# Windowed attention ahead of two feed-forward nets: global keys between K^T's blocks, quarter-array products in two banks, ten weight pieces begun in listed steps

## The chip, the core and the metric

The kernel runs on one core of one Trainium2 chip. The metric is the device time of one execution in microseconds. The core has five engines that each run their own list in order: PE (TensorE, with its weight loads shown as PEld), DVE (VectorE), ACT (ScalarE), POOL (GpSimd) and SP, which here only issues transfers. All numbers are fp32.

## The reference, cut to what matters

Four batches, eight heads, 512 local and 32 global positions per head, head size 64. A local query sees the keys within 32 positions and the 32 global keys; a global query sees all 544 keys. The 2176 x 512 result goes through two nets of width 2048.

```python
k_all = np.concatenate([k_g, k_l], axis=2)
out_g = np.matmul(sm(scale * np.matmul(q_g, k_all.transpose(0, 1, 3, 2))), v_all)
s_ll  = np.where(np.abs(pos[:, None] - pos[None, :]) <= 32, scale * q_l @ k_l.T, -1e9)
a_l   = sm(np.concatenate([scale * q_l @ k_g.T, s_ll], axis=-1))
out_l = np.matmul(a_l, np.concatenate([v_g, v_l], axis=2))
x = concat([out_g, out_l], axis=2).transpose(0, 2, 1, 3).reshape(2176, 512)
x = (h * cos(h)) @ w_out      with h = x @ w_in        # first net
y = relu(h)**2 @ w_out        with h = x @ w_in        # second net
```

## The kernel before, in words

**Items and steps.** The attention is cut into 40 items: 32 `Local` ones (a pair of heads and one half of the 512 positions) and 8 `Global` ones (four heads), always four Locals and then a Global. Steps -3 to 43 run through them. In each step the list `CFG["order"]` sets in which order the stages are written, and `CFG["lag"]` says for which item: S (scores) for item s, SM (maxima on DVE, exponentials on ACT) for s, RC and NM (reciprocal; scaling, most of it on POOL) for s-1, TM (transposes of the probabilities on PE) for s-2, TE (their copies out of PSUM, by ACT) for s-3, OM and OE (products with V, and the copy of the result) for s-4. Global items stand at the steps 4, 9, 14 and so on. Each engine runs its part strictly in the order written.

**K^T.** `tr_k` (TRK) transposes the keys of a head pair, `k_evac` (KEV, ACT) copies them as eight blocks of 64 into `kT`, eight rows of 160: block, next block, 32 global keys. `k_copy` (KC, POOL) fills the other two parts: line 351 copies the next blocks (448 columns), line 353 the global keys (256 columns), line 361 the last 64 keys.

**Products.** `o_mm` makes two 128-column halves `i`. For each it issues two products with the global values (line 504: 128 rows against 64 columns of the array, 128 columns wide) and four with the local values (line 516). Results of one item lie in one of the banks 6 and 7, in turn, and `o_evac` copies 256 columns with one DVE instruction (line 529), after NM and the weight conversion in DVE's order.

**Loads.** SP issues K loads (LK) in the steps 0, 5, 10, ... 25, Q loads (LQ) in 1, 6, 11, ... 26, V loads (LV) in 8, 13, ... 33, and copies of V shifted by 64 rows (CV) in 11, 16, ... 36; every tenth step from 5 on it also loads `vgz`.

**Weights.** The nets' weights come in 64 pieces of 512 KB. `Feed.begin` issues the load of a piece (`raw`) and shifts a list of stages: two steps later ACT and POOL read it (`conv_a`, lines 146 and 143), three steps later DVE (`conv_b`, lines 154 and 155), four steps later POOL (`conv_c`, line 165). `begin` stands (BG) behind LQ and TE, ahead of LK and of the exponentials. Before, half a credit per step from step 5 on, with none in the steps five ahead of a head pair, begins pieces in the steps 8, 11, 14, 18, 21, 24, 28, 31, 34, 36 and 38, and from step 40 on one in nearly every step. `Feed.split`, in listed steps, makes two-part weights of converted pieces.

From step 40 on `ffn_step` runs the nets as well: products `h` (line 757) and `y` (line 786).

Of the kernel before, what the change touches and what calls it, by code (L numbers as in the profile page):

```python
# [26 lines left out]
           'RC', 'NM', 'CB', 'LV', 'OE', 'TRQ', 'QE', 'KC', 'TM'],  # L27
# [19 lines left out]
 'free': -5,  # L47
 'kb': 'P',
 'split': [22, 24, 27, 29, 33],
 'sx': [32, 34, 37, 39],  # L50
 'arate': 0.5,
 'rate': 0.5,
 's0': 5,
# [6 lines left out]
RATE, ARATE, XD, NRING = CFG["rate"], CFG["arate"], CFG["xd"], CFG["nr"]  # L60

@with_exitstack
def kernel(
# [250 lines left out]
    def load_vg(b):  # L314
        for u in range(4):
            nc.sync.dma_start(
                VGZ[b % 2][32 * u : 32 * u + 32, :, u, :],
                v_g[b].rearrange("(k h) p d -> p k h d", h=2)[:, :, u // 2, :],
            )

    def tr_k(p):
        b, kk = divmod(p, NPAIR)
        tk = bank(BT, "tk")
        for c in range(4):
            nc.tensor.transpose(  # L325
                tk[:, c * P : (c + 1) * P],
                kn[p // 2][:, c, 2 * (p % 2) : 2 * (p % 2) + 2].rearrange("p h d -> p (h d)"),
                ident,
            )
        t = ep.tile([P, 8, KTB], F32, tag="kT", name="kT", bufs=3)  # L330
        kT[p] = t
        tks[p] = tk

    def k_evac(p):
        t, tk = kT[p], tks.pop(p)
        nc.scalar.activation(
            t[:, :, 0:64], tk.rearrange("p (j q) -> p j q", q=64), AF.Copy
        )
        if CFG["kb"] == "A":
            nc.scalar.activation(  # L340
                t[:, :, 128:KTB], tk[:, 0:SG].unsqueeze(1).to_broadcast([P, 8, SG]), AF.Copy
            )
        elif CFG["kb"] == "D":
            nc.vector.tensor_copy(
                t[:, :, 128:KTB], tk[:, 0:SG].unsqueeze(1).to_broadcast([P, 8, SG])
            )

    def k_copy(p):
        t = kT[p]
        one = dict(scalar1=1.0, scalar2=1.0, op0=ALU.mult, op1=ALU.mult)  # L350
        nc.gpsimd.tensor_scalar(t[:, 0:7, 64:128], t[:, 1:8, 0:64], **one)
        if CFG["kb"] == "P":
            nc.gpsimd.tensor_scalar(
                t[:, :, 128:KTB], t[:, 0, 0:SG].unsqueeze(1).to_broadcast([P, 8, SG]), **one
            )
        if p > 1:
            k_tail(p)

    def k_tail(p):
        b, kk = divmod(p, NPAIR)  # L360
        nc.gpsimd.tensor_scalar(
            kT[p][:, 7, 64:128], ktail[:, kk, b, :], 1.0, 1.0, op0=ALU.mult, op1=ALU.mult
        )
# [41 lines left out]

    class Local:
# [19 lines left out]

        def softmax(self):
            self.pt = lp.tile([P, 4, KTB], F32, tag="pt", name="pt", bufs=4)  # L430
            self.st = lp.tile([P, 3, 4], F32, tag="st", name="st", bufs=4)

            def unit(u):
                i = 2 * self.hb + u % 2
                m = masks[1] if i == 0 else masks[2] if i == 3 else masks[0]
                nc.vector.tensor_tensor_reduce(  # L436
                    out=self.pt[:, u, :],
                    in0=self.s[u // 2][:, 160 * (u % 2) : 160 * (u % 2) + 160],
                    in1=m,
                    scale=-0.125,  # L440
                    scalar=3.0e38,
                    op0=ALU.add,
                    op1=ALU.min,
                    accum_out=self.st[:, 0, u : u + 1],
                )
# [9 lines left out]
            return [lambda u=u: unit(u) for u in range(4)]  # L455
# [10 lines left out]
        def norm(self):  # L466
# [3 lines left out]
                self.pt[:, :, P:KTB],  # L470
# [54 lines left out]
        def o_evac(self):  # L525
            c0 = self.b * SL + 256 * self.hb
            dst, src = xt[:, self.kk, c0 : c0 + 256], self.o.rearrange("p i q -> p (i q)")
            if CFG["oe"][self.hb] == "D":
                nc.vector.tensor_copy(dst, src)
            else:  # L530
                nc.scalar.activation(dst, src, AF.Copy)


    class Global:
# [3 lines left out]
        def s_mm(self):  # L538
            self.s = []
            for n in (320, 256):  # L540
                s = bank(BT if CFG["sgb"] >> (n == 256) & 1 else BS, "sg")
                self.s.append(s)
                for i in range(2):
# [5 lines left out]
                        rhs=t[:, 0:5, 0:64] if n == 320 else t[:, 5:8:2, 0:128],  # L549
# [64 lines left out]
        def o_mm(self):  # L614
            self.o = bank(BO, "og")[:, 0 : 2 * SG].rearrange("p (i q) -> p i q", i=2)
# [33 lines left out]
    for h in range(2):  # L649
# [6 lines left out]
            out=masks[0][s, 64:128], in_=masks[0][s, 64:128], pattern=[[-1, 64]],  # L656
# [5 lines left out]
    nc.vector.memset(masks[2][64:128, 96:128], NEG)  # L662
# [361 lines left out]
```

## Time and profile before

| what | us |
|---|---|
| three runs, median (lowest to highest) | 913.23 (912.32 to 914.58) |
| the profiled execution's own time | 911.74 |
| its span, first to last instruction | 910.0 |
| PE busy in the span | 890.7 |
| DVE, ACT, POOL busy | 502.5, 439.4, 447.8 |
| first product of the nets starts at | 146.06 |

Busy is time in which an engine has an instruction in hand; it doesn't say that the engine is at its best rate. What counts for the end is in which stretch PE has to wait, or has work that could be shorter. PEclk is the share of the full TensorE clock that was granted: 1.00 is 2.4 GHz, 0.5 is 1.2 GHz.

### The profile page before, as it was taken

To read this page: it belongs to the slowest core of one execution; us is meant where nothing else is said; L and a number is where in the kernel's file an instruction comes from. 1 tells how busy PE (TensorE), PEld (TensorE's weight loads), DVE (VectorE), ACT (ScalarE), POOL (GpSimd) and SP (SyncE) were. 2 spreads that over 40 slices of the span, in tenths; PEclk is the share of its full clock that TensorE was granted. 3 is DMA by queue.
4 is the path that set the end of the run, shared out by engine and by line. 5 is a ranking of instruction groups with operands and counts; after the bars stand their busy time and mean duration, and the time that the engine had idled before them with its cause. 6 is when DMAs were issued, how large, how long until landed. Compare 5 with 4: busy or idle time off the path is not lost.

```text
span 910.0 us, 15436 instructions
## 1 busy us (share of the span) xinstructions
PE 890.7 (98%) x5720; PEld 793.7 (87%) x5720; DVE 502.5 (55%) x1058; ACT 439.4 (48%) x1036; POOL 447.8 (49%) x517
## 2 busy tenths in 40 slices
PE   7899999999999999999999999999999999999997
PEld 5777777999999999999999988889999888899996
DVE  5687899866776666765554483433422833232221
ACT  5778787665655545545444553333334632222211
POOL 4577888754574435744342484444423842222221
PEclk9999999999999999999999999999999999999999
DMA  7888643221122111121110021111100101010001
GB/s 168 192 192 195 165 129 94 71 70 53 49 62 70 47 53 61 50 70 47 47 47 1 1 70 47 53 44 66 47 1 1 47 1 47 1 47 1 35 35 36
DMA packets 82075, 57.10 MB, mean 63 GB/s; under 512 B 58320, under 2 KB 74704, under 8 KB 82000
## 3 DMA queue, kind: packets, MB, share of 16 engines
q1 hardware_dynamic: 79824, 55.59, 22.0%
q8 instruction: 45, 0.74, 0.3%
q10 hardware_dynamic: 2176, 0.52, 0.3%
q14 instruction: 30, 0.25, 0.1%
HBM read 47.45 MB, written 4.46 MB: 57 GB/s over the span
## 4 chain that ended last, share of the span: by engine, by line
PE 91%; DVE 3%; DMA 2%; ACT 1%; SPq 1%; POOL 1%; issue 1%; ACTq 0%; POOLq 0%; DVEq 0%
PE h L757 41%; PE y L786 41%; PE s L420 2%; PE tw L488 1%; PE o L504 1%; PE tq L368 1%; DVE pt L436 1%; PE o L516 1%; PE og L622 1%; DMA raw<-in_moe_w_out_dram 1%; PE sg L546 1%; PE tk L325 0%; ACT pt L446 0%; SPq L292 0%; PE twg L603 0%
## 5 line engine op out<-in xcount | busy, mean ns | idle before, releaser
L757 PE MATMUL h<-x,w 128*128 128x436 f32 (+3 forms) x1920 | 403.4, 358 | 0.0
L857 POOL TENSOR_TENSOR glo<-cr,ghi 128x436 fp32r<-128x436 f32 (+3 forms) x160 | 186.8, 1167 | 407.7 <-ACT ghi L851 393.9
L757 PEld LDWEIGHTS h<-x,w 128*128 128x128 f32 x1920 | 354.6, 188 | 27.5
L786 PE MATMUL y<-ghi,w 128*128 128x436 f32 (+1 forms) x640 | 177.6, 358 | 0.0
L846 DVE TENSOR_TENSOR cr<-h,cr 128x436 f32<-128x436 f32 (+3 forms) x160 | 96.6, 605 | 134.0 <-ACT cr L837 115.0
L786 PE MATMUL y<-w,ghi 128*128 128x512 f32 x544 | 168.4, 390 | 0.0
L745 DVE TENSOR_TENSOR x<-xt,x 128x436 fp32r<-128x436 f32 (+3 forms) x100 | 102.5, 1035 | 93.3 <-ACT x L744 78.3
L837 ACT ACTIVATE cr<-h 128x384 f32<-128x384 f32 (+1 forms) x80 | 42.8, 535 | 210.7 <-PE h L757 209.4
L786 PEld LDWEIGHTS y<-ghi,w 128*128 128x128 f32 x640 | 120.3, 188 | 6.1
L786 PEld LDWEIGHTS y<-w,ghi 128*128 128x128 f32 x544 | 101.4, 188 | 18.9
L786 PE MATMUL y<-glo,w 128*128 128x436 f32 (+1 forms) x320 | 114.8, 359 | 0.0
L786 PE MATMUL y<-w,glo 128*128 128x512 f32 x272 | 106.8, 393 | 0.0
L851 ACT ACTIVATE ghi<-cr 128x436 fp32r<-128x436 f32 (+3 forms) x160 | 89.7, 560 | 24.5 <-DVE cr L846 23.6
L831 ACT ACTIVATE ck<-h 128x436 int32<-128x436 f32 (+1 forms) x80 | 42.6, 532 | 113.1 <-PE h L757 113.1
L833 DVE SCALAR_TENSOR_TENSOR cr<-h,ck 128x436 f32<-128x436 f32 (+1 forms) x80 | 48.6, 607 | 84.9 <-ACT ck L831 84.9
L165 POOL TENSOR_TENSOR r<-cu,cc 128x512 uint32<-128x512 uint32 x64 | 85.0, 1328 | 2.0 <-DVE cc L155 2.0
L744 ACT ACTIVATE x<-xt 128x436 fp32r<-128x436 f32 (+3 forms) x100 | 55.1, 560 | 20.2 <-PE h L757 19.9
L786 PEld LDWEIGHTS y<-glo,w 128*128 128x128 f32 x320 | 60.1, 188 | 2.7
L786 PEld LDWEIGHTS y<-w,glo 128*128 128x128 f32 x272 | 51.0, 188 | 10.8
L842 ACT ACTIVATE cr<-cr,halfpi 128x436 f32<-128x436 f32 (+1 forms) x80 | 52.5, 657 | 10.1 <-DVE cr L833 10.1
L155 DVE SCALAR_TENSOR_TENSOR cc<-raw,cc 128x512 uint32<-128x512 uint32 x64 | 55.7, 870 | 0.0
L446 ACT ACTIVATE pt<-pt,st 128x160 f32<-128x160 f32 x128 | 53.3, 425 | 4.1 <-DVE st L436 4.1
(91 smaller groups left out, 907.4 us busy)
## 6 DMA issues: line engine op xcount, KB each, us to landing
raw<-in_moe_w_in_dram SPq DMA_DIRECT2D x32, 512.0 KB, 3.7
raw<-in_moe_w_out_dram SPq DMA_DIRECT2D x32, 512.0 KB, 3.5
vb<-va SPq DMA_DIRECT2D x16, 256.0 KB, 4.6
out_dram<-ypart SPq DMA_DIRECT2D x16, 256.0 KB, 2.1
qn<-in_q_l_dram SPq DMA_DIRECT2D x28, 128.0 KB, 3.7
va<-in_v_l_dram SPq DMA_DIRECT2D x24, 128.0 KB, 3.3
kn<-in_k_l_dram SPq DMA_DIRECT2D x21, 128.0 KB, 3.0
va<-in_v_l_dram SPq DMA_DIRECT2D x8, 96.0 KB, 3.2
```

Of the source, the lines that this page charges most:

```text
L155: lambda: v.scalar_tensor_tensor(c, t[:, :, 1].bitcast(U32), 0x80000000, c, op0=ALU.bitwise_and, op1=ALU.bitwise_or,),
L165: nc.gpsimd.tensor_tensor(ring[g][:, q, :].bitcast(U32), u, c, op=ALU.add)
L446: nc.scalar.activation(self.pt[:, u, :], self.pt[:, u, :], AF.Exp, bias=self.st[:, 0, u : u + 1], scale=-1.0, accum_out=self.st[:, 1, u : ...
L744: nc.scalar.activation(hi, xr, AF.Copy)
L745: return lambda: (nc.vector if kk in XD else nc.gpsimd).tensor_tensor(lo, xr, hi.bitcast(F32), op=ALU.subtract)
L757: nc.tensor.matmul(h, lhsT=w[:, ws, 0, kk * P : (kk + 1) * P], rhs=x, start=(k == 0), stop=(k == 3 * NK - 1),)
L786: nc.tensor.matmul(o, lhsT=l, rhs=r, start=(c_first and k == 0), stop=(c_last and k == 2))
L833: lambda: nc.vector.scalar_tensor_tensor(r, h, INV2PI, k, op0=ALU.mult, op1=ALU.subtract),
L842: nc.scalar.activation(ctmp[s], ctmp[s], AF.Sin, bias=halfpi, scale=TWOPI)
L846: nc.vector.tensor_tensor(r, hps.pop(s), r, op=ALU.mult)
L851: nc.scalar.activation(ghi[s], ctmp[s], AF.Copy)
L857: nc.gpsimd.tensor_tensor(lo, ctmp.pop(s), hi.bitcast(F32), op=ALU.subtract)
```

## The change

**K^T** becomes nine rows of 96: block, 32 global keys. A query block's 160 keys are then one contiguous run, block j, global keys, block j+1, so line 351 goes, and the masks and the slices of the probabilities move with it. The scaled probabilities go to a tile of their own, `pn`, and `pt` has three buffers of five rows.

**Products.** The four products with the global values come first, each on 64 rows and 64 columns of the array; the two row halves write different banks. Each item now uses a 128-column half of both banks 6 and 7, and the halves alternate. `o_evac` is two copies of 128 columns, and OE moves ahead of RC, right behind the maxima.

**Weights.** Pieces begin in the ten steps listed under `begin`, and none at BG from step 37 on. The split steps are 15, 21, 25, 31 and 35.

```diff
@@ CFG
- 'order': [... 'SM', 'RC', 'NM', 'CB', 'LV', 'OE', 'TRQ', 'QE', 'KC', 'TM'],
+ 'order': [... 'SM', 'OE', 'RC', 'NM', 'CB', 'LV', 'TRQ', 'QE', 'KC', 'TM'],
- 'split': [22, 24, 27, 29, 33],
+ 'split': [15, 21, 25, 31, 35],
- 'arate': 0.5,
+ 'begin': [6, 9, 14, 16, 19, 24, 26, 29, 34, 36],
@@ pools
+    obank = [ps.tile([P, 512], F32, tag=f"bank{k}", name="o") for k in BO]
+    def out_half():
+        k = turn["o"] = turn.get("o", 1) ^ 1
+        return [t[:, P * k : P * k + P] for t in obank]
+    GK = slice(64, 64 + SG)
@@ k_copy
-        nc.gpsimd.tensor_scalar(t[:, 0:7, 64:128], t[:, 1:8, 0:64], **one)
-        if CFG["kb"] == "P":
-            nc.gpsimd.tensor_scalar(
-                t[:, :, 128:KTB], t[:, 0, 0:SG].unsqueeze(1).to_broadcast([P, 8, SG]), **one
-            )
+        nc.gpsimd.tensor_scalar(
+            t[:, 0:8, GK], t[:, 0, 0:SG].unsqueeze(1).to_broadcast([P, 8, SG]), **one
+        )
@@ Local.s_mm
-                            rhs=kT[self.p][d, j, :],
+                            rhs=kT[self.p].rearrange("p j q -> p (j q)")[d, 96 * j : 96 * j + KTB],
@@ Local.norm
+            self.pn = lp.tile([P, 4, P], F32, tag="pn", name="pn", bufs=2)
-                    self.pt[:, u, 0:P],
-                    self.pt[:, u, 0:P],
+                    self.pn[:, u].rearrange("p (a q) -> p a q", a=2),
+                    windows(self.pt, u),
@@ Local.o_mm
-            self.o = bank(BO, "o")[:, 0:256].rearrange("p (i q) -> p i q", i=2)
+            self.o = out_half()
             for i in range(2):
+                r = slice(64 * i, 64 * i + 64)
                 for h in range(2):
                     nc.tensor.matmul(
-                        self.o[64 * h : 64 * h + 64, i, :],
-                        lhsT=VGZ[self.b % 2][:, self.kk, 2 * h + i, :],
-                        rhs=self.tgs,
+                        self.o[i][64 * h : 64 * h + 64],
+                        lhsT=VGZ[self.b % 2][r, self.kk, 2 * i + h, :],
+                        rhs=self.tgs[r],
@@ Local.o_evac
-            dst, src = xt[:, self.kk, c0 : c0 + 256], self.o.rearrange("p i q -> p (i q)")
-            if CFG["oe"][self.hb] == "D":
-                nc.vector.tensor_copy(dst, src)
+            for i in range(2):
+                nc.vector.tensor_copy(xt[:, self.kk, c0 + P * i : c0 + P * i + P], self.o[i])
@@ steps
-                cb = feed.begin(ARATE if due(CFG["free"]) is None else 0.0) if s >= CFG["s0"] else []
+                cb = feed.begin(1.0 if s in CFG["begin"] else 0.0)
```

SP's list before, from the Q loads (`qn`) of step 6 on; `raw` is the first weight piece, begun in step 8, `va` the V loads of step 8:

```order
L292 DMA qn<-in_q_l_dram 128x4x64 x4
L397 DMA qgn<-in_q_g_dram 32x8x64
L126 DMA raw<-in_moe_w_in_dram 128x4x256
L299 DMA va_85<-in_v_g_dram 32x4x64
L302 DMA va_85<-in_v_l_dram 96x4x64
```

The same stretch of SP's list now:

```order
L299 DMA qn<-in_q_l_dram 128x4x64 x4
L124 DMA raw<-in_moe_w_in_dram 128x4x256
L394 DMA qgn<-in_q_g_dram 32x8x64
L306 DMA va_87<-in_v_g_dram 32x4x64
L309 DMA va_87<-in_v_l_dram 96x4x64
```

The first piece moved ahead of one 64 KB load, and is issued right behind the four Q loads of step 6, not ahead of them.

ACT's list before, from the copies (`tws`, `tgs`) of step 8 on; the exponentials are `pt`, `cc` is the first reader of `raw`:

```order
L494 ACTIVATE tws<-tw 128x512
L498 ACTIVATE tgs<-tg 128x128
L446 ACTIVATE pt,st<-pt,st 128x160 x4
L494 ACTIVATE tws<-tw 128x512
L498 ACTIVATE tgs<-tg 128x128
L336 ACTIVATE kT<-tk 128x8x64
L571 ACTIVATE ptg,stg<-sg,stg 128x320
L571 ACTIVATE ptg,stg<-sg,stg 128x224
L494 ACTIVATE tws<-tw 128x512
L498 ACTIVATE tgs<-tg 128x128
L146 ACTIVATE cc<-raw 128x512
```

ACT's list now, from the same copies of step 8 on:

```order
L498 ACTIVATE tws<-tw 128x512
L502 ACTIVATE tgs<-tg 128x128
L144 ACTIVATE cc<-raw 128x512
L449 ACTIVATE pt,st<-pt,st 128x160 x4
L498 ACTIVATE tws<-tw 128x512
L502 ACTIVATE tgs<-tg 128x128
L343 ACTIVATE kT<-tk 128x8x64
L574 ACTIVATE ptg,stg<-sg,stg 128x320
```

The reader of the first piece moved two steps up, from step 10 to step 8, ahead of that step's exponentials.

PE's list before, a step with a Local's scores (`s`), its products (`o`) and the transposes of Q (`tq`), with waits:

```order
L420 MATMUL s<-kT,qT 64x160 x6
L504 MATMUL o<-tgs,vgz_89 64x128 x2
L516 MATMUL o<-tws,va_86 64x64 [waits DMAHW5_49]
L516 MATMUL o<-tws,va_86 64x64
L516 MATMUL o<-tws,vb_88 64x64 x2
L504 MATMUL o<-tgs,vgz_89 64x128 x2
L516 MATMUL o<-tws,va_86 64x64 x2
```

The same step now:

```order
L423 MATMUL s<-kT,qT 64x160 x6
L509 MATMUL o<-tgs,vgz_91 64x128 [waits DVE_49]
L509 MATMUL o<-tgs,vgz_91 64x128
L509 MATMUL o<-tgs,vgz_91 64x128 [waits DVE_49]
L509 MATMUL o<-tgs,vgz_91 64x128
L522 MATMUL o<-tws,va_88 64x64 [waits DMAHW5_49]
L522 MATMUL o<-tws,va_88 64x64
```

The four products with the global values stand together, and the first of each bank has a wait on DVE that was not there.

## Rows read from the trace of the kernel before

**Rows 1.** Busy time by stretch (us: engine busy (instructions), PEclk, DMA share, GB/s)

```profile
core 0: us, PE busy (x) PEld busy (x) DVE busy (x) ACT busy (x) POOL busy (x), PEclk, DMA share, GB/s
20.00:33.00 13.00, 10.46 (x149) 8.17 (x152) 8.51 (x45) 8.16 (x33) 6.21 (x16) 1.00 0.88 197
...
42.00:59.00 17.00, 15.78 (x254) 12.59 (x253) 13.10 (x63) 13.34 (x51) 11.83 (x27) 1.00 0.87 196
59.00:75.00 16.00, 16.00 (x258) 13.07 (x257) 13.41 (x64) 12.95 (x51) 13.39 (x27) 1.00 0.91 201
...
126.00:143.00 17.00, 14.85 (x241) 11.27 (x239) 16.32 (x68) 13.77 (x52) 14.72 (x26) 1.00 0.41 125
...
161.00:910.00 749.00, 743.93 (x3651) 678.11 (x3649) 375.38 (x540) 319.76 (x609) 332.06 (x288) 1.00 0.13 42
```

**Rows 2.** Chain that ended last, one Local's products (start us, us, what)

```profile
66.42 0.37 PE o L504 x4
...
67.02 0.22 PE o L504 x4
```

**Rows 3.** Groups by line (busy us, mean ns | idle before, releaser)

```profile
L529 DVE COPY xt<-o 128x256 f32<-128x256 f32 x32 | 13.2, 413 | 1.4 <-PE o L516 1.4
...
L351 POOL TENSOR_SCALAR kT<-kT 128x448 f32<-128x448 f32 x16 | 9.4, 588 | 4.5 <-ACT kT L336 4.5
...
L633 DVE COPY xt<-og 128x64 f32<-128x64 f32 x8 | 1.7, 214 | 0.0
```

**Rows 4.** Timeline of PE and POOL at the nets' start (start, us, what, idle before)

```profile
145.87 0.33 PE L488 MATMUL tw<-ident,pt 128*128 128x128 f32 x1 [0.37 <-POOL pt L475]
...
143.71 2.10 POOL L475 TENSOR_SCALAR pt<-pt,st 128x128 f32<-128x128 f32 x3
```

**Rows 5.** Timeline of ACT, step 13: the reader of a piece waits

```profile
55.92 0.69 ACT L146 ACTIVATE cc<-raw 128x512 uint32<-128x512 uint32 x1 [2.17 <-DMA raw<-in_moe_w_out_dram]
```

**Rows 6.** Timeline of SP, Q loads of step 6 and the first piece

```profile
34.75 2.59 SPq L292 DMA_DIRECT2D qn<-in_q_l_dram  x4
...
37.94 1.34 SPq L126 DMA_DIRECT2D raw<-in_moe_w_in_dram  x1
```

**Rows 7.** Tile raw, the one load issued between 37.5 and 39 us

```profile
DMA to landing us min/median/max: 5.1/5.1/5.1
```

**Rows 8.** Timeline of ACT, behind step 8's copies and step 9's copy

```profile
38.06 0.43 ACT L446 ACTIVATE pt<-pt,st 128x160 f32<-128x160 f32 x1
...
39.71 0.59 ACT L494 ACTIVATE tws<-tw 128x512 f32<-128x512 f32 x1
```

**Rows 9.** Timeline of PE, step 9's transposes

```profile
41.72 0.60 PE L488 MATMUL tw<-ident,pt 128*128 128x128 f32 x4
```

**Rows 10.** Timeline of SP, Q loads of step 16

```profile
65.94 3.09 SPq L292 DMA_DIRECT2D qn<-in_q_l_dram  x4
```

**Rows 11.** Tile raw, the one load issued at 69.75 us

```profile
DMA to landing us min/median/max: 5.2/5.2/5.2
```

**Rows 12.** Timeline of ACT, behind step 18's copies

```profile
70.88 0.43 ACT L446 ACTIVATE pt<-pt,st 128x160 f32<-128x160 f32 x1
```

**Rows 13.** Timeline of SP and ACT, step 26's Q loads and step 28's copies

```profile
98.61 3.27 SPq L292 DMA_DIRECT2D qn<-in_q_l_dram  x4
...
105.57 0.42 ACT L446 ACTIVATE pt<-pt,st 128x160 f32<-128x160 f32 x1
```

**Rows 14.** Busy time in a stretch with the lower clock (columns as in rows 1)

```profile
87.00:92.00 5.00, 4.51 (x35) 3.32 (x37) 3.03 (x10) 3.45 (x13) 2.65 (x8) 0.66 0.68 153
```

**Rows 15.** Timeline of SP and ACT, the piece begun in step 21

```profile
81.92 0.50 SPq L126 DMA_DIRECT2D raw<-in_moe_w_in_dram  x1
...
87.49 0.67 ACT L146 ACTIVATE cc<-raw 128x512 uint32<-128x512 uint32 x1
```

**Rows 16.** Timeline of DVE, step 12's last maximum

```profile
50.70 0.32 DVE L436 CUSTOM_DVE_ANT_0 pt<-s,mask 128x160 f32<-128x160 f32 x1
```

**Rows 17.** Timeline of PE, step 13's scores

```profile
51.30 0.77 PE L420 MATMUL s<-kT,qT 64*64 64x160 f32 x16
```

More of the change, by code (lines that the diff above doesn't have):

```diff
@@ L26 @@
 CFG = {'order': ['CV', 'LQ', 'S', 'TE', 'BG', 'LK', 'OM', 'TRK', 'KEV', 'CC', 'SM',
-           'RC', 'NM', 'CB', 'LV', 'OE', 'TRQ', 'QE', 'KC', 'TM'],
+           'OE', 'RC', 'NM', 'CB', 'LV', 'TRQ', 'QE', 'KC', 'TM'],
  'lag': {'S': 0,
@@ L46 @@
  'teg': 'AA',
- 'free': -5,
  'kb': 'P',
- 'split': [22, 24, 27, 29, 33],
+ 'split': [15, 21, 25, 31, 35],
  'sx': [32, 34, 37, 39],
- 'arate': 0.5,
+ 'begin': [6, 9, 14, 16, 19, 24, 26, 29, 34, 36],
  'rate': 0.5,
- 's0': 5,
  'groups': [[4, 5, 7], [8, 8]],
@@ L59 @@
 GROUPS = CFG["groups"]
-RATE, ARATE, XD, NRING = CFG["rate"], CFG["arate"], CFG["xd"], CFG["nr"]
+RATE, XD, NRING = CFG["rate"], CFG["xd"], CFG["nr"]
 @with_exitstack
@@ L317, in load_vg @@
                 VGZ[b % 2][32 * u : 32 * u + 32, :, u, :],
-                v_g[b].rearrange("(k h) p d -> p k h d", h=2)[:, :, u // 2, :],
+                v_g[b].rearrange("(k h) p d -> p k h d", h=2)[:, :, u % 2, :],
             )
@@ L329, in tr_k @@
             )
-        t = ep.tile([P, 8, KTB], F32, tag="kT", name="kT", bufs=3)
+        t = ep.tile([P, 9, 64 + SG], F32, tag="kT", name="kT", bufs=3)
         kT[p] = t
@@ L336, in k_evac @@
         nc.scalar.activation(
-            t[:, :, 0:64], tk.rearrange("p (j q) -> p j q", q=64), AF.Copy
+            t[:, 0:8, 0:64], tk.rearrange("p (j q) -> p j q", q=64), AF.Copy
         )
-        if CFG["kb"] == "A":
-            nc.scalar.activation(
-                t[:, :, 128:KTB], tk[:, 0:SG].unsqueeze(1).to_broadcast([P, 8, SG]), AF.Copy
-            )
[L343 to L346, printed above, removed]
     def k_copy(p):
@@ L361, in k_tail @@
         nc.gpsimd.tensor_scalar(
-            kT[p][:, 7, 64:128], ktail[:, kk, b, :], 1.0, 1.0, op0=ALU.mult, op1=ALU.mult
+            kT[p][:, 8, 0:64], ktail[:, kk, b, :], 1.0, 1.0, op0=ALU.mult, op1=ALU.mult
         )
@@ L403, in load_qgn, with windows @@
         load_small(qgn, q_g[b], b)
+    def windows(t, u):
+        return t.rearrange("p u q -> p (u q)")[:, KTB * u : KTB * u + 192].rearrange(
+            "p (a q) -> p a q", a=2
+        )[:, :, 0:64]
     class Local:
@@ L429, in softmax @@
         def softmax(self):
-            self.pt = lp.tile([P, 4, KTB], F32, tag="pt", name="pt", bufs=4)
+            self.pt = lp.tile([P, 5, KTB], F32, tag="pt", name="pt", bufs=3)
             self.st = lp.tile([P, 3, 4], F32, tag="st", name="st", bufs=4)
             def unit(u):
-                i = 2 * self.hb + u % 2
+                i = 2 * self.hb + u // 2
                 m = masks[1] if i == 0 else masks[2] if i == 3 else masks[0]
@@ L437, in unit @@
                     out=self.pt[:, u, :],
-                    in0=self.s[u // 2][:, 160 * (u % 2) : 160 * (u % 2) + 160],
+                    in0=self.s[u % 2][:, 160 * (u // 2) : 160 * (u // 2) + 160],
                     in1=m,
@@ L453, in unit @@
                 )
-            return [lambda u=u: unit(u) for u in range(4)]
+            return [lambda u=u: unit(u) for u in (0, 2, 1, 3)]
         def recip(self):
@@ L469, in norm @@
                 self.pg,
-                self.pt[:, :, P:KTB],
+                self.pt[:, 0:4, GK],
                 self.st[:, 2, :].unsqueeze(2).to_broadcast([P, 4, SG]),
@@ L487, in t_mm @@
             for u in range(4):
-                nc.tensor.transpose(self.tw[:, u, :], self.pt[:, u, 0:P], ident)
+                nc.tensor.transpose(self.tw[:, u, :], self.pn[:, u], ident)
             nc.tensor.transpose(self.tg, self.pg.rearrange("p u q -> p (u q)"), ident)
@@ L516, in o_mm @@
                         nc.tensor.matmul(
-                            self.o[64 * h : 64 * h + 64, i, q],
+                            self.o[i][64 * h : 64 * h + 64, q],
                             lhsT=v[:, 2 * self.hb + i, 2 * (self.p % 2) + h, :],
-                            rhs=self.tws[:, 2 * h + i, q],
+                            rhs=self.tws[:, 2 * i + h, q],
                             start=False,
@@ L526, in o_evac @@
             c0 = self.b * SL + 256 * self.hb
-            dst, src = xt[:, self.kk, c0 : c0 + 256], self.o.rearrange("p i q -> p (i q)")
-            if CFG["oe"][self.hb] == "D":
-                nc.vector.tensor_copy(dst, src)
-            else:
-                nc.scalar.activation(dst, src, AF.Copy)
+            for i in range(2):
+                nc.vector.tensor_copy(xt[:, self.kk, c0 + P * i : c0 + P * i + P], self.o[i])
     class Global:
@@ L548, in s_mm @@
                         lhsT=qgbd[:, kk, self.b, :],
-                        rhs=t[:, 0:5, 0:64] if n == 320 else t[:, 5:8:2, 0:128],
+                        rhs=t[:, 0:5, 0:64] if n == 320 else t[:, 5:9, 0:64],
                         start=True,
@@ L614, in o_mm @@
         def o_mm(self):
-            self.o = bank(BO, "og")[:, 0 : 2 * SG].rearrange("p (i q) -> p i q", i=2)
+            self.o = out_half()[0][:, 0 : 2 * SG].rearrange("p (i q) -> p i q", i=2)
             va = VA[(2 * self.b + self.g) % 2]
@@ L655 @@
         nc.gpsimd.affine_select(
-            out=masks[0][s, 64:128], in_=masks[0][s, 64:128], pattern=[[-1, 64]],
+            out=masks[0][s, 96:160], in_=masks[0][s, 96:160], pattern=[[-1, 64]],
             compare_op=ALU.is_ge, fill=NEG, base=0, channel_multiplier=1,
@@ L661 @@
     nc.vector.memset(masks[1][0:64, 0:32], NEG)
-    nc.vector.memset(masks[2][64:128, 96:128], NEG)
+    nc.vector.memset(masks[2][64:128, 128:160], NEG)
     nc.vector.memset(qgbd, 0.0)
```

1 line of the change is left out of this document (removed).

## The prediction

> **What bounds the kernel now.** I began with the busy time by stretch [rows 1]. From 161 to 910 us PE is busy 743.93 of 749 us: there the nets are bound by their products, which the change does not touch. So what counts is when the first product of the nets begins (146.06 us). Ahead of it three regimes follow one another. From 20 to 33 us the loads are the limit: PE has 10.46 us of work in 13 while the DMA engines are at 0.88. From 42 to 75 PE is the limit: 15.78 of 17 and 16.00 of 16 us busy. From 126 to 143 DVE is: 16.32 of 17, against 14.85 of PE. Next I read the chain of waits for one Local's products [rows 2], the groups by line for the removed and split copies [rows 3], and the timelines around each piece that is begun at a new step [rows 5 to 13]. In those the reader should look at three times: when SP has issued the load, when it lands, and when ACT, which works strictly in order, stands at its reader.
>
> **Products by quarters.** The chain shows the two pairs of global products of a Local as 0.37 and 0.22 us [rows 2]. As four quarters in one block they occupy the array at the same time, so the second pair goes: 0.22 us a Local. Bounds: 0 if quarters run one pair after the other, 32 x 0.37 = 11.8 us if a whole pair's lead-in goes too. I take 0.22, the row of the pair that is dropped. It counts only where PE is the limit. Of 32 Locals 4 lie in the load-bound stretch and 6 in the DVE-bound one, so 22 x 0.22 = **-4.8 us**.
>
> **K^T.** Line 351 goes: 16 x 0.588 = 9.4 us of POOL [rows 3]. POOL is busy 11.83 of 17 and 13.39 of 16 us in the stretches that PE sets [rows 1], so this is hidden: 0. The scores keep their width of 160 columns.
>
> **Two copies behind the maxima.** A copy of 256 columns takes 413 ns, one of 64 columns 214 [rows 3]; between them 128 columns are about 0.28 us, so two take 0.56 instead of 0.41: +0.15 x 32 = 4.8 us of DVE. In 42 to 75 DVE has over 2 us free in 16 [rows 1], which hides it. In 126 to 143, where DVE is the limit, 7 Locals would cost 1.0, but a piece's conversion leaves that stretch (the last four pieces begin earlier or not at all there), worth about as much: 0, bounds -1 to +1. The copies also move ahead of the reciprocal, which makes the scaling on POOL 0.56 us later; POOL's spare time above covers it.
>
> **The new wait.** Both banks are used by every item, so the global products of a step wait until DVE has copied the step before. In step 12 the last maximum ends at 50.70 + 0.32 = 51.02 [rows 16]; two copies more end at 51.58. Step 13's scores run from 51.30 for 0.77 us, to 52.07 [rows 17], and only then come its products. So 0.5 us are spare and I take **0**. Behind the wait PE holds the transposes and the next scores, and ACT and DVE wait for those; the price if the spare time is gone is in rival C.
>
> **The pieces that begin in new steps.** This is the largest term. SP issues its loads in a fixed order. In step 6 the piece now goes out right behind the four Q loads. Those are issued until 34.75 + 2.59 = 37.34 [rows 6]; the first piece of before, issued at 37.94, took 5.1 us to land [rows 6, 7]. So it lands at 37.34 + 5.1 = 42.44. Its reader stands two steps later, in step 8, ahead of the exponentials, where ACT arrives at 38.06 [rows 8]: a wait of 4.4 us. ACT then does the conversion, 0.69 us [rows 5], before the exponentials. How much of that reaches PE? The copy of the transposes that PE waits for next ended at 39.71 + 0.59 = 40.30 [rows 8], and PE wrote its next ones at 41.72 [rows 9]: 1.42 us spare. So 4.4 + 0.69 - 1.42 = 3.7 us. I try this formula on before's own step 13, where the reader waited 2.17 us [rows 5]: 2.17 + 0.69 - 1.42 = 1.4, and PE's idle time in 42 to 59 is 1.22 [rows 1]. It holds.
>
> In step 16 the Q loads end at 65.94 + 3.09 = 69.03 [rows 10], the piece lands 5.2 later [rows 11], at 74.23, and ACT is at its reader at 70.88 [rows 12]: wait 3.35, on PE 3.35 + 0.69 - 1.42 = 2.6. By then ACT is itself late by 3.7 - 1.2 - 8 x 0.22 = 0.7 (the last two are worked out below and above); if SP does not share that, 1.9 is left, and without the spare time it is 4.0. I keep 2.6. In step 26 the Q loads end at 98.61 + 3.27 = 101.88; with 5.1 to land that is 106.98 against 105.57 [rows 13]: wait 1.4, on PE 0.7 at most; the DMA engines are less loaded by then (0.68 in [rows 14]), so I take half, 0.3. The other pieces begin behind V loads or where ACT comes later; 0. Together 3.7 + 2.6 + 0.3 = **+6.6 us**, bounds 0 and 9.8 (4.4 + 0.69, 3.35 + 0.69 and 0.7, nothing hidden).
>
> **What the move removes.** Before's wait in step 13 goes, since the second piece now begins in step 9: **-1.2** (PE's idle time, [rows 1]). At the start of the nets PE's last transposes of probabilities wait for POOL, whose scaling took 2.10 us at 143.71 [rows 4], the mean of three being stretched by a conversion on DVE beside it. No conversion falls there now, and I take half of the 2.10 back: **-1.0**, bounds 0 and -2.1.
>
> **The clock.** In 87 to 92 us the granted clock was 0.66 of 2.4 GHz, a mean of the two levels, behind a stretch with waits [rows 14]; it cost at most (1 - 0.66) x 5 = 1.7 us. Two new stretches in which PE has little to do for 3 us each may bring one or two such drops in place of this one. I take **+0.8**, bounds 0 and 3.4 - 1.7 = 1.7.
>
> The Trainium skill, "TensorE: Matmul & The Clock Gate", section "HAM oscillation — how this bites in real kernels", says that waits for DMA between short bursts of products drop PE to the lower clock, and that this is paid each time. It speaks against this change, and the row of the one drop agrees in kind.
>
> **Sum.** 6.6 + 0.8 - 4.8 - 1.2 - 1.0 = +0.4 on the profiled execution's own 911.74, whose span is 910.0: 912.1. The median of the three runs is 1.5 above the profiled one, so **913.6 us**: the gain in the products is given back by two readers that stand before their data.
>
> **Rivals.** *B, the pieces land in time: faster.* For it: before itself began a piece in a Q step, issued at 81.92, and its reader at 87.49 started without a wait [rows 15]. SP may also run further ahead once POOL and PE are quicker. Against it: that reader came 5.6 us after the issue, while the new ones come 0.7 and 1.9 us after it [rows 6, 8, 10, 12]. Then the waits go and so does the one clock drop: -4.8 - 1.2 - 1.0 - 1.6 = -8.6, that is 903.1 + 1.5 = 904.6.
>
> *C, the copies hold the products: slower.* One mechanism: DVE ends a step's copies after PE has ended the next scores, which begins where DVE is over 0.5 us later than in step 12. Where DVE is late for half of the Locals by 0.4 beyond that, it costs 16 x 0.4 = 6.4: 920.0. For it: DVE's list is busy 13.10 of 17 us [rows 1], and a copy that follows four maxima is never early. Against it: the spare time worked out above, in the stretch that counts.
>
> The order of PE's list shows the waits on DVE. The Trainium skill, "PSUM — Partial Sum Buffer", section "PSUM bank collisions raise a hardware error", gives the rule behind them: two engines must not touch one bank in the same partitions at once, even at different columns. By it, alternating halves of two shared banks buys no overlap between the copy and the next products; no run shown here tests that.
>
> *D, the waits at their upper end, with two clock drops: slower.* 9.8 + 1.7 - 7.0 = +4.5 gives 917.7. It holds if nothing is spare behind the late exponentials, because the next step's maxima are late too.
>
> *E, the quarters do not overlap: the change does not do what it says.* The 4.8 us stay: 918.4. Against it: the two heads of a pair, on different columns, already run side by side [rows 2].
>
> **How the numbers follow.** Forecast 0.42, B 0.30, C 0.09, D 0.15, E 0.04. What this kernel's measurements can tell from no change is about 0.3%, 2.7 us. So faster 0.30, same 0.42, slower 0.28. The range goes from 904.0, just below B, to 918.5, just above D and E; what is outside is most of C, the lower part of B and the worst of D, 2 in 10. The forecast's own range is 910.5 to 916.
>
> **What the profile after would show.** Right: in steps 8 and 18 ACT idle for 3 to 4.5 us ahead of its reader at line 144, released by the load, and PE idle 2 to 4 us soon after; no wait in step 13; four global products in one block of about 0.2 us for a Local instead of 0.37 and 0.22; copies of 128 columns near 0.28 us; the nets' first product within 2 us of 146.06. Wrong by B: ACT's readers start without a wait and the first product is near 138. Wrong by C: waits of the first global products on DVE of 0.3 us or more, step after step. Wrong by D: two or more stretches at a lower granted clock between 40 and 80 us. A change inside the nets, past 161 us, would make the whole reading wrong.

## The result, and the profile after

The changed kernel takes 926.1 us (924.31 to 927.02, four runs), the one before 912.78 in the same comparison: a ratio of 1.0141, interval 1.012 to 1.0162. The forecast was 913.6 and the range ended at 918.5. The profiled execution's span went from 910.0 to 924.8 us. The nets' first product, at 146.06 before, starts here:

```profile
159.57 1.04 PE L760 MATMUL h<-x,w 128*128 128x436 f32 x4
```

So 13.5 of the 14.9 us arose ahead of the nets. By stretch, as in [rows 1] (busy time and instructions of each engine, PEclk, DMA share, GB/s):

```profile
core 0: us, PE busy (x) PEld busy (x) DVE busy (x) ACT busy (x) POOL busy (x), PEclk, DMA share, GB/s
...
33.00:42.00 9.00, 9.00 (x131) 7.12 (x129) 5.41 (x31) 5.01 (x21) 3.49 (x10) 0.84 0.82 198
42.00:59.00 17.00, 13.65 (x199) 10.73 (x196) 10.69 (x53) 11.74 (x45) 9.61 (x20) 0.80 0.76 171
59.00:75.00 16.00, 15.06 (x245) 11.65 (x248) 12.74 (x66) 13.32 (x50) 9.72 (x23) 1.00 0.64 137
75.00:87.00 12.00, 7.86 (x114) 5.79 (x114) 7.38 (x27) 6.77 (x27) 7.20 (x14) 0.86 0.94 227
...
110.00:126.00 16.00, 12.92 (x196) 9.77 (x188) 11.38 (x51) 10.85 (x44) 11.35 (x24) 0.85 0.75 190
```

From 42 to 59, where PE was busy 15.78 us before, it is busy 13.65, at a mean clock of 0.80. The timeline of ACT names the cause: three readers of a piece, in the steps 8, 18 and 28, wait for their load, as the reader of [rows 5] did for 2.17 us.

```profile
44.51 0.66 ACT L144 ACTIVATE cc<-raw 128x512 uint32<-128x512 uint32 x1 [4.32 <-DMA raw<-in_moe_w_in_dram]
...
82.41 0.66 ACT L144 ACTIVATE cc<-raw 128x512 uint32<-128x512 uint32 x1 [5.23 <-DMA raw<-in_moe_w_out_dram]
...
119.10 0.66 ACT L144 ACTIVATE cc<-raw 128x512 uint32<-128x512 uint32 x1 [4.20 <-DMA raw<-in_moe_w_in_dram]
```

A step later PE stands behind ACT's next copy of the transposes; that is where [rows 9] ran without a wait. The timeline of PE (the first line is the wait for the last keys in step 6, which was there before too, but 1.75 us long and with the clock at 1.00 behind it; now the clock is 0.84 from 33 to 42 us, and e11 below shows what such a hole costs):

```profile
31.51 0.40 PE L377 MATMUL ttail<-ident,ktn 32*128 32x32 f32 x4 [3.11 <-DMA ktn<-in_k_l_dram]
...
47.34 1.11 PE L492 MATMUL tw<-ident,pn 128*128 128x128 f32 x4 [3.35 <-ACT tws L498]
...
85.25 1.11 PE L492 MATMUL tw<-ident,pn 128*128 128x128 f32 x4 [4.14 <-ACT tws L498]
...
121.94 1.12 PE L492 MATMUL tw<-ident,pn 128*128 128x128 f32 x4 [3.08 <-ACT tws L498]
```

Note that the four transposes behind a hole last 1.11 us, against 0.60 in [rows 9]. Fine stretches around the first and the second hole show why: PE at work throughout, at the lower level of 0.50 (1.2 GHz). Behind the third the clock is 0.50 too, from 122 to 126 us.

```profile
41.00:45.00 4.00, 3.00 (x39) 1.72 (x37) 2.29 (x8) 0.49 (x1) 0.45 (x1) 1.00 0.70 194
45.00:48.00 3.00, 0.66 (x3) 0.66 (x4) 1.02 (x4) 3.00 (x13) 2.22 (x7) 0.67 0.97 211
48.00:52.00 4.00, 4.00 (x47) 3.15 (x46) 2.59 (x14) 3.10 (x14) 3.43 (x6) 0.50 1.17 256
...
86.00:90.00 4.00, 4.00 (x47) 3.15 (x46) 2.89 (x15) 3.10 (x14) 3.67 (x7) 0.50 1.13 225
```

Two smaller terms. The copies of 128 columns, beside [rows 3], and POOL's scaling at the nets' start, beside [rows 4], with the conversion that DVE runs meanwhile:

```profile
L534 DVE COPY xt<-o 128x128 f32<-128x128 f32 x64 | 16.0, 284 | 4.5 <-PE o L522 3.9
```

```profile
157.22 2.10 POOL L479 TENSOR_SCALAR pn<-pt,st 128x128 f32<-128x128 f32 x3
...
157.44 0.68 DVE L153 SCALAR_TENSOR_TENSOR cc<-raw,cc 128x512 uint32<-128x512 uint32 x1
...
158.33 0.33 PE L492 MATMUL tw<-ident,pn 128*128 128x128 f32 x1 [0.53 <-POOL pn L479]
```

The copies are as estimated. The scaling still takes 2.10 us, with a conversion on DVE beside it as before, and PE still waits for it.

### The profile page after: what moved, and what is told of

It reads as the page before. It is cut to its first block, busy times and chain, and to the rows that moved or that the text cites. A ratio compares the mean times of both kernels' runs of the same rounds, so it can differ in the third digit from the quotient of the medians.

```text
span 924.8 us, 15435 instructions
## 1 busy us (share of the span) xinstructions
PE 896.0 (97%) x5720; PEld 792.5 (86%) x5720; DVE 504.9 (55%) x1090; ACT 439.8 (48%) x1036; POOL 441.3 (48%) x501
## 4 chain that ended last, share of the span: by engine, by line
PE 87%; DMA 4%; ACT 2%; DVE 2%; SPq 2%; issue 1%; POOL 1%; ACTq 0%; POOLq 0%
PE h L760 41%; PE y L789 41%; DMA raw<-in_moe_w_in_dram 1%; PE o L522 1%; PE s L423 1%; PE tw L492 1%; ACT pt L449 1%; DMA ktn<-in_k_l_dram 1%; DMA qn<-in_q_l_dram 1%; DVE pt L439 1%; DMA raw<-in_moe_w_out_dram 1%; DMA vb<-va 1%; SPq L309 1%; PE o L509 1%; POOL pn L479 1%
## 5 line engine op out<-in xcount | busy, mean ns | idle before, releaser
L748 DVE TENSOR_TENSOR x<-xt,x 128x436 fp32r<-128x436 f32 (+3 forms) x100 | 109.3, 1105 | 95.9 <-ACT x L747 80.9
L789 PEld LDWEIGHTS y<-w,glo 128*128 128x128 f32 x272 | 51.0, 188 | 10.7
L141 POOL TENSOR_SCALAR cu<-raw 128x512 f32<-128x512 f32 x64 | 50.7, 792 | 13.3 <-DMA raw<-in_moe_w_in_dram 8.4
```

Of the source, the lines that this page charges most:

```text
L141: nc.gpsimd.tensor_scalar(u, t[:, :, 1].bitcast(F32), 2.0**-112, 1.0, op0=ALU.mult, op1=ALU.mult)
L748: return lambda: (nc.vector if kk in XD else nc.gpsimd).tensor_tensor(lo, xr, hi.bitcast(F32), op=ALU.subtract)
L789: nc.tensor.matmul(o, lhsT=l, rhs=r, start=(c_first and k == 0), stop=(c_last and k == 2))
```

## The experiments

Theory T: the readers that stand before their data, and the clock behind them, are the whole loss. Rival R: the shared banks, the two copies and the waits on DVE have a good part in it. Times are medians; `before` was run beside each group, at 911.5 (e1 to e4), 912.2 (e5 to e8) and 912.1 (e9 to e12), so runs of different groups are better compared by their ratio to before.

### Which part of the change: e1, e2, e3

e1 is the changed kernel with the begin and split steps of before:

```diff
- 'split': [15, 21, 25, 31, 35],
+ 'split': [22, 24, 27, 29, 33],
- 'begin': [6, 9, 14, 16, 19, 24, 26, 29, 34, 36],
+ 'begin': [8, 11, 14, 18, 21, 24, 28, 31, 34, 36, 38],
```

> The changed kernel, with the weight pieces begun in the steps of before (8, 11, 14, 18, 21, 24, 28, 31, 34, 36, 38) and its split steps; everything else is as changed. Theory T (the readers that stand before their data, and the lower clock behind them, are the whole loss; the rest of the change gains): no ACT reader waits over 2.5 us, the one wait of step 13 comes back, the first product of the nets is at 141 to 143 us, 907 to 910 us. Rival R (shared banks, two copies behind the maxima and the waits on DVE are a good part of the loss): first product later than 148 us, 915 us or more.

Measured: 912.59 us, ratio to before 1.0019 (1.0004 to 1.0033). The nets begin at 144.87. No reader waits over 1.3 us.

e2 moves three pieces only:

```diff
- 'begin': [6, 9, 14, 16, 19, 24, 26, 29, 34, 36],
+ 'begin': [8, 9, 14, 18, 19, 24, 28, 29, 34, 36],
```

> The changed kernel with only three entries of its list moved: pieces of steps 6, 16 and 26 begin in 8, 18 and 28. Theory T: the waits of 4.32, 5.23 and 4.20 us at ACT's reader go, PE loses 3.35 + 4.14 + 3.08 us of idle time and the three stretches at half clock, so 926.1 - 10.6 - 6 = 909.5, between 906 and 911 us. Rival R: under half of it goes, 918 us or more. Third possibility: two pieces in successive steps make a new wait of 2 us or more at the reader of the second one, 911 to 916 us.

Measured: 913.6 us, 1.0029 (1.0013 to 1.0046). That lies in the third possibility's range, but its sign is missing: the longest wait of a reader is 0.17 us, and the nets begin at 146.28. e3 is the other way round, the kernel before with the new list:

```diff
- cb = feed.begin(ARATE if due(CFG["free"]) is None else 0.0) if s >= CFG["s0"] else []
+ cb = feed.begin(1.0 if s in CFG["begin"] else 0.0)
```

(with `begin` and `split` of the change).

> The kernel before with only the begin steps and split steps of the change; K^T, products, banks and copies are those of before. Theory T: the same three waits appear at ACT (4 to 5 us each), with the clock at a half behind each, and no gain of the quarters to set against them: 926 to 931 us. Rival R: 913 to 919 us, with most of the loss missing.

Measured: 922.84 us, 1.0125 (1.0101 to 1.015), between the two ranges. The clock falls less there than in the changed kernel (a mean of 0.90 from 42 to 59 us, against 0.80). ACT waits in the same way, for instance:

```profile
43.80 0.66 ACT L147 ACTIVATE cc<-raw 128x512 uint32<-128x512 uint32 x1 [5.80 <-DMA raw<-in_moe_w_in_dram]
...
80.93 0.66 ACT L147 ACTIVATE cc<-raw 128x512 uint32<-128x512 uint32 x1 [4.19 <-DMA raw<-in_moe_w_out_dram]
```

Three list entries thus carry the loss: putting them back gives 12.5 us (e2), the whole list 13.5 (e1), and the list costs 11.4 in the kernel before (e3). R falls as an explanation of the slowdown. But T missed too: e1 and e2 came out 2.6 us above the top of its ranges, level with before or a little slower, and e3 3 us under its range. The rest of the change gains next to nothing.

### The load's place or the reader's: e9

The list stays, and so does SP's order to the last row. Only the readers stand one step later:

```diff
- self.stage = [None] * 5
+ self.stage = [None] * 6
- a, b, c = self.stage[2:]
+ a, b, _ = self.stage[3:]
- c = self.stage[4]
+ c = self.stage[5]
```

> The changed kernel with its own list of begin steps, so every load stands on SP exactly where the change puts it; only the readers of a piece stand one step later each (ACT and POOL three steps behind the begin, DVE four, POOL's last five). Theory T (the reader's place ahead of the exponentials is the loss, not the load's place): waits at ACT of 4.3, 5.2 and 4.2 us shrink by a step of 2.3 to 3.4 us each, to 1 to 3 us, the clock stays up, 912 to 916 us. Rival L (the pieces ahead of the V loads of steps 8, 18, 28 hold up the loads that attention needs): 921 us or more.

Measured: 915.43 us, 1.0032 (1.0017 to 1.0047). This is in T's range, and L is out: 10.7 of the 13.3 us are back with SP's list unchanged, so it is the reader's place. What is left of the waits, on ACT:

```profile
43.28 0.69 ACT L144 ACTIVATE cc<-raw 128x512 uint32<-128x512 uint32 x1 [1.69 <-DMA raw<-in_moe_w_in_dram]
...
75.78 0.67 ACT L144 ACTIVATE cc<-raw 128x512 uint32<-128x512 uint32 x1 [2.17 <-DMA raw<-in_moe_w_out_dram]
...
107.88 0.69 ACT L144 ACTIVATE cc<-raw 128x512 uint32<-128x512 uint32 x1 [1.02 <-DMA raw<-in_moe_w_in_dram]
```

The granted clock is 1.00 behind all three.

### What the clock costs by itself: e4, e12, e11

e4 leaves the waits of the changed kernel and gives PE something to do in them; the added products feed nothing:

```diff
+ if c == "TM" and s in (9, 19, 29):
+     for _ in range(13):
+         nc.tensor.matmul(
+             obank[0][:, 256:384], lhsT=ident, rhs=ident,
+             start=True, stop=True, skip_group_check=True,
+         )
```

> The changed kernel with 13 extra products of 128x128 by 128x128 ahead of the transposes in steps 9, 19 and 29, where PE stands idle for 3.35, 4.14 and 3.08 us; their results go to columns of a bank that nothing reads. They take some 3 us of each hole. Theory T2 (the lower clock behind a hole costs time by itself, about 2 us each): the granted clock stays at 1.00 in the 8 us behind each hole, and 926.1 - 6 = 918 to 921 us. Rival: the clock is only a sign of the waiting, and the steps behind a hole are limited by something else: 925 to 928 us whatever the clock shows.

Measured: 919.66 us, 1.0091 (1.0076 to 1.0106), 6.4 us less than the changed kernel for 39 extra products. The added work and the clock:

```profile
43.65 3.07 PE L960 MATMUL o<-ident 128*128 128x128 f32 x26
```

```profile
42.00:59.00 17.00, 16.97 (x275) 14.34 (x271) 13.55 (x65) 14.52 (x57) 12.43 (x25) 1.00 0.78 158
...
75.00:87.00 12.00, 11.62 (x169) 9.43 (x173) 8.77 (x37) 9.04 (x34) 8.60 (x15) 1.00 1.08 230
```

ACT still waits there, 3.64 us at the first reader and then

```profile
77.42 0.68 ACT L144 ACTIVATE cc<-raw 128x512 uint32<-128x512 uint32 x1 [3.74 <-DMA raw<-in_moe_w_out_dram]
...
112.50 0.68 ACT L144 ACTIVATE cc<-raw 128x512 uint32<-128x512 uint32 x1 [3.85 <-DMA raw<-in_moe_w_in_dram]
```

and the clock stays at 1.00. So the lower clock is no mere sign of waiting. It costs some 2 us a hole on average: four us of work at 0.50, as in the row from 48 to 52 above. It is not even: from the first reader to the second the profiled execution is 4.1 us shorter than the changed kernel's, of which 1.5 is the shorter wait at the second reader, from there to the third 1.6, and to the nets 1.5. What the holes cost without the clock is the distance from e4 to e2, 919.66 - 913.6 = 6.1 us, though PE's idle time in the changed kernel's three adds up to 10.6 us.

e12 leaves one of the three pieces where the change puts it:

```diff
- 'begin': [6, 9, 14, 16, 19, 24, 26, 29, 34, 36],
+ 'begin': [8, 9, 14, 16, 19, 24, 28, 29, 34, 36],
```

> The changed kernel with the pieces of steps 6 and 26 begun in 8 and 28, but that of step 16 where the change has it. Theory T (each hole has its own price, hole plus the clock behind it): ACT waits 4 to 5 us in step 18 only, PE 3 to 4 us, and 913.6 of e2 + 4.1 + 2 = 918 to 920.5 us. Rival (later slack absorbs a single hole): 914 to 916 us.

Measured: 915.39 us, 1.0032 (1.0016 to 1.0047), under what T gave and in the rival's range. A single late reader waits less than the same one behind an earlier hole:

```profile
73.89 0.69 ACT L144 ACTIVATE cc<-raw 128x512 uint32<-128x512 uint32 x1 [3.28 <-DMA raw<-in_moe_w_out_dram]
```

```profile
76.76 0.88 PE L492 MATMUL tw<-ident,pn 128*128 128x128 f32 x4 [2.17 <-ACT tws L498]
```

The 3.28 us are what the prediction's formula gave for this reader (3.35), and PE's 2.17 are near its 2.6. In the profiled execution, 912.23 us, the clock did not fall behind that hole. The ten executions go with this: two with a mean granted clock of 0.997 took 912.2 and 912.6, the eight with 0.992 to 0.995 took 914.5 to 917.3; only the first has a trace. There the nets begin at 145.17, no later than in e2 (146.28), so in this execution the hole by itself cost nothing at the end. The holes' prices do not simply add.

e11 fills the hole of step 6 in e1, where the clock had been 0.85 from 33 to 42 us:

```diff
+ if s == 6:
+     for _ in range(10):
+         nc.tensor.matmul(obank[0][:, 256:384], lhsT=ident, rhs=ident, ...)
```

> e1 with 10 extra products (about 2.4 us) in the hole of 2.50 us in step 6, where PE waits for the last keys; the granted clock behind it was 0.85 over 9 us. Theory M (the clock costs time only where PE is the limit; up to some 40 us the loads are): the clock is 1.00 behind the hole and the time is e1's within 1 us, 911.6 to 913.6. Rival (a lower clock costs its lost cycles wherever it falls): 1.3 us less and more, 911 or under.

Measured: 914.11 us, 1.0019 (1.0006 to 1.0032). The median is over both ranges, but the ratio is e1's, so there is no gain. The clock is 1.00 and PE comes on faster, only to reach the next late piece:

```profile
33.00:42.00 9.00, 9.00 (x154) 7.16 (x154) 6.63 (x35) 6.81 (x30) 4.96 (x14) 1.00 0.76 180
```

```profile
56.37 0.69 ACT L144 ACTIVATE cc<-raw 128x512 uint32<-128x512 uint32 x1 [3.25 <-DMA raw<-in_moe_w_out_dram]
```

That reader, of step 13, waited 1.30 us in e1. So in this stretch, where the loads set the pace, the lower clock cost nothing that can be seen.

### Why the rest gains so little: e5, e10, e6

e5 is e1 with whole-row products, all else kept:

```diff
- lhsT=VGZ[self.b % 2][r, self.kk, 2 * i + h, :], rhs=self.tgs[r],
+ lhsT=VGZ[self.b % 2][:, self.kk, 2 * i + h, :], rhs=self.tgs,
```

> e1 (the changed kernel with the begin steps of before) with the global products on all 128 rows instead of quarters; banks, copies and order stay as changed. Theory Q (the quarters save 0.22 us where they follow scores, and give 0.10 back where they follow a Global's scores, since the weights of another tile shape start later): the block gets longer by some 0.2 us for a Local, the nets begin 2 to 4 us later than in e1 (144.9), 914.5 to 916.5 us. Rival (the banks and copies hide any saving): within 1 us of e1's 912.6. Apart from that: in before the nets take 763.9 us from their first product to the end, in all variants of the changed kernel 765.3; if the quarters' shape is what sets that, it is 763.9 here.

Measured: 914.1 us, 1.0026 (1.0014 to 1.0039), and the nets begin at 147.10, 2.2 us later than in e1. In time the difference is 1.5 us by the medians, but 0.6 by the ratios to before, whose intervals overlap: it is not clear of noise. One Local behind its scores, e5 and then e1:

```profile
66.98 0.77 PE L423 MATMUL s<-kT,qT 64*64 64x160 f32 x16
67.68 0.66 PE L509 MATMUL o<-tgs,vgz 128*64 128x128 f32 x8
...
68.73 0.66 PE L332 MATMUL tk<-ident,kn 128*128 128x128 f32 x4
```

```profile
65.97 0.77 PE L423 MATMUL s<-kT,qT 64*64 64x160 f32 x16
66.56 0.40 PE L509 MATMUL o<-tgs,vgz 64*64 64x128 f32 x8
...
67.50 0.33 PE L332 MATMUL tk<-ident,kn 128*128 128x128 f32 x1
```

From scores to transposes 1.75 against 1.53 us: the 0.22 forecast from [rows 2]. Behind a Global's scores it is otherwise. PE and its weight loads in e1:

```profile
72.22 1.19 PE L549 MATMUL sg<-kT,qgbd 128*64 128x320 f32 x8
...
73.34 0.21 PEld L509 LDWEIGHTS o<-tgs,vgz 64*64 64x64 f32 x8 [0.39 <-issue]
73.34 0.45 PE L509 MATMUL o<-tgs,vgz 64*64 64x128 f32 x8
...
74.33 0.42 PEld L332 LDWEIGHTS tk<-ident,kn 128*128 128x128 f32 x4
```

The quarters' weights start 0.39 us late behind products of another shape, and the block takes 2.11 us up to the next transposes. e10 uses whole rows in those eight steps alone:

```diff
- r = slice(64 * i, 64 * i + 64)
+ r = slice(0, P) if whole else slice(64 * i, 64 * i + 64)
+ elif c == "OM" and isinstance(i, Local):
+     i.o_mm(isinstance(it(s), Global))
```

> e1 with whole-row products in the 8 steps where they follow a Global's scores, quarters in the other 24. Theory Q: the block there goes back from 2.12 to 2.02 us, counted from the Global's scores to the next transposes, 0.8 us in all at most: 911.5 to 913 us, not to be told from e1. Rival (the tile shape's change has nothing to do with it): the block grows by 0.2 us as in the other Locals, 914 us.

```profile
73.00 1.19 PE L549 MATMUL sg<-kT,qgbd 128*64 128x320 f32 x8
73.81 0.58 PEld L509 LDWEIGHTS o<-tgs,vgz 128*64 128x64 f32 x8
...
75.02 0.42 PEld L332 LDWEIGHTS tk<-ident,kn 128*128 128x128 f32 x4
```

The gap is gone and the block takes 2.02 us, as expected; the time, 913.25 us and 1.0006 (0.9987 to 1.0024), is between the two ranges and can't be told from e1's or from before. The shape's change explains one Local in four.

e6 keeps only the new K^T and the tile `pn`; `o_mm`, the banks, the one copy of 256 columns and the place of OE are those of before.

> e1 with the products, the banks, the single copy of 256 columns and the place of that copy as before: of the change only K^T's layout and the tile of scaled probabilities are left. Theory K (the layout costs and saves nothing on the path): 911 to 913 us, with the nets' first product at 146 plus or minus 1. Rival (POOL freed of 9.4 us shortens the attention): first product before 144.5, under 910.5 us. The nets from first product to end: 763.9 us if quarters, banks or copies set the pace, 765.3 if the layout in memory does.

Measured: 913.17 us, 1.0024 (1.0011 to 1.0036), nets from 147.73, a little later than theory K gave. POOL's 9.4 us buy nothing, as forecast. Between e5 and e6 lie the banks, the copies and OE: 0.9 us, less than the spread of either. So these cost nothing that can be seen.

### The load stream takes back what is gained: e7, e8

In both kernels one load moves, the first of the last keys (`ktn`), in e1 and in before:

```diff
- if s in (4, 14, 24):
+ if s in (1, 14, 24):
      load_ktn(s // 10 + 1)
```

> e1 with the first load of the last keys (ktn, 64 KB) issued in step 1 ahead of the V loads, not in step 4 behind them. In e1 PE stands idle 2.50 us for it in step 6, and the granted clock is 0.85 over the 9 us behind. Theory H (in the load-bound beginning a faster kernel only waits longer at the next load, and then pays for the clock too): both go, 2.5 + 1.3 = 3.8 us less at most, 908.5 to 910.5 us. Rival (the next load, of K or V, takes its place): under 1 us less, 911.6 to 913 us.

> The kernel before with the same move of one load. There PE waits 1.75 us in step 6 and the clock stays at 1.00 behind it. Theory H: 1 to 1.8 us less, 909.7 to 910.5 us by 911.5 of before. Rival (the next load takes its place): no change, 911 to 912 us.

Measured: 914.51 us (1.0037, 1.0021 to 1.0054) and 913.33 us (1.0017, 1.0 to 1.0034). Nothing is gained in either, as the rival said; the medians are even 1.5 and 1.3 us over its ranges, with e8's interval still touching no change. The wait in step 6 is gone, and a longer one comes in step 13 (4.03 us on PE in e8), with the clock after it. In e7:

```profile
59.56 0.69 PE L492 MATMUL tw<-ident,pn 128*128 128x128 f32 x2 [3.43 <-ACT tws L498]
```

```profile
59.00:75.00 16.00, 15.44 (x221) 12.41 (x223) 12.02 (x59) 12.68 (x51) 10.62 (x20) 0.80 0.79 172
```

Up to some 60 us SP issues loads almost without a pause (the gaps of over 0.3 us add up to 1.4 us in before and 2.4 in e1). In both trials what came earlier on PE was waited off at the next load.

## Why the prediction was wrong, point by point

- **The mechanism of the largest term was right.** Pieces behind Q loads, readers two steps later ahead of the exponentials, waits of 4.4 and 3.35 us: the first was 4.32, and PE lost 3.35 of the 3.7 forecast.
- **The waits in steps 18 and 28 were too small:** 5.23 and 4.20 us on ACT, 4.14 and 3.08 on PE, where the text had 3.35 and 1.4, 2.6 and 0.3. In step 18 ACT stood at its reader at 82.41 - 5.23 = 77.18, only 0.7 us behind the end of the Q loads at 76.46, not 1.9, and the load took 5.8 us to land, not 5.2:

```profile
73.41 3.05 SPq L299 DMA_DIRECT2D qn<-in_q_l_dram  x4
```

```profile
DMA to landing us min/median/max: 5.8/5.8/5.8
```

  The lost margin goes with the clock: in e4, where it stays up behind the first hole, ACT is 1.9 us behind the Q loads (73.68 and 71.77) and waits 3.74. In step 28 ACT stood at its reader at 119.10 - 4.20 = 114.90, 2.4 us behind the end of the Q loads at 112.51, not 3.7, and the load took 6.4 us to land, not the 5.1 carried over from [rows 7]:

```profile
109.98 2.53 SPq L299 DMA_DIRECT2D qn<-in_q_l_dram  x4
112.68 0.38 SPq L124 DMA_DIRECT2D raw<-in_moe_w_in_dram  x1
```

```profile
DMA to landing us min/median/max: 6.4/6.4/6.4
```

  The 3.7 was read from a trace in which PE had been held up just before (the stretch of [rows 14]). Other traces fit this, but no run tests it alone: e8, which is before with one load moved and has no drop there, shows 2.2 us, and e6, which has one, 4.2.

  e12, where no such hole came before, showed 3.28 us for step 18: the formula was right for one late reader and wrong for a row of them. Its last part, from ACT's wait to PE, held: 4.32, 5.23 and 4.20 + 0.69 - 1.42 give 3.6, 4.5 and 3.5, and PE lost 0.2 to 0.4 less.
- **The clock was the step that failed most.** The text took +0.8, at most +1.7; e4 measured 6.4. It priced "one or two such drops in place of this one", at the size of the one drop in [rows 14], though the sum itself put waits of over 2 us into two places where PE then has a full list. The sentence cited there from the Trainium skill, "TensorE: Matmul & The Clock Gate", section "HAM oscillation — how this bites in real kernels", said that waits for DMA are paid for again each time at the lower clock. The trace agrees: 0.50 behind each of the three. This row of evidence against the change was named and then given almost no weight.
- **The quarters** save 0.22 us where forecast, so rival E is out, but 0.6 to 1.5 us in all (e5 against e1, not clear of noise), not 4.8. One Local in four gives 0.10 back. That the rest is lost where the loads or DVE set the pace is likely, but not shown.
- **The two credits** did not come. The wait of step 13 went, but in e1 it is back at 1.30 us on ACT and costs PE nothing, and e2, without it, is no faster than e1: no run shows the -1.2 in time. The scaling at the nets' start kept its 2.10 us: 0, not -1.0. The text said that no conversion falls there now; the trace has DVE's at 157.44, beside POOL's scaling.
- **Held as forecast:** K^T 0, the copies' duration (0.284 us), and no measurable cost of the waits on DVE, so rival C is out. Whether two engines may share a bank in time, the rule cited there from the Trainium skill, "PSUM — Partial Sum Buffer", no run tried. Rival B is out, since the readers waited. Rival D came nearest, with 10.6 us of waits on PE against 9.8, but not by its mechanism: it holds if nothing is spare behind the late exponentials, and 1.7 to 1.8 us were (4.32 + 0.69 - 3.35 in the first). Its clock was too small by 4.7, and of the lower stretches that it looked for between 40 and 80 us only one began there.
- **The nets themselves** were to stay as they were. They take 1.4 us longer (see the last section). The text named a change in there as a sign that the whole reading is wrong; 1.4 of 14.9 us is too little for that.

Put together by the runs: the changed kernel lies 6.4 us over e4 (the clock, forecast 0.8), e4 6.1 over e2 (the waits, forecast 6.6), and e2 0.8 over before's 912.78, or 2.1 by the before of its own group (the gains, forecast -7.0). So the waits' price in time was near the forecast, although PE's idle time was 10.6 us; that is in part luck, since the waits in the later steps grew with the clock and e12 shows that the parts depend on each other. What failed is the clock, by 5.6 us, and the gains, of which none is left in time.

## What to carry to other kernels

An early load is only half a prefetch: a reader at a fixed distance on an in-order engine must be timed from when its load can land, not from when it is begun, and moving the reader by one step was worth 10.7 us here with the order of the loads unchanged. Where a wait makes PE stand still, price the hole and the lower clock behind it as two terms, and do so for each hole: here the clock cost as much as the holes. A margin between two engines read from a trace of before can shrink when one of them is held up at another place: 1.9 us became 0.7 behind the first hole.

## What was not expected of the hardware

The nets take 763.9 us from their first product to the end in before and e3, and 765.2 to 765.3 in the changed kernel and all its variants. PE is busy throughout in both, from 180 to 200 us for instance, but gets through 105 products in before and 103 in e1:

```profile
180.00:200.00 20.00, 20.00 (x105) 19.42 (x104) 13.65 (x23) 11.99 (x24) 10.80 (x10) 1.00 0.17 53
```

```profile
180.00:200.00 20.00, 20.00 (x103) 19.00 (x102) 13.67 (x21) 11.68 (x23) 12.02 (x11) 1.00 0.16 54
```

Product follows product every 0.1933 us in the first, 0.1978 in the second, at the same granted clock. In before the faster pace lasts for about the first 430 products, up to some 217 us; then it runs at 0.1978 too. e8, which differs from before in the place of one load, never has the faster pace (765.3 us). So the slower pace needs neither the quarters nor the layout. What sets it stays open, also whether it belongs to the kernel or to the execution, as each kernel has one trace. It is worth 1.4 us in these executions, as much as the 1.2 us by which e1's nets begin earlier.
